# Decode block with gradients on one core: block-diagonal products on VectorE or GpSimd, two rows kept on chip, and a new order of the work

## The chip, the cores and the metric

The kernel runs on one core of a Trainium2 chip. The core has five engines that run beside each other: PE (TensorE, matrix products into PSUM), DVE (VectorE), ACT (ScalarE), POOL (GpSimd) and SP (SyncE, which here only issues transfers), and 16 DMA engines that move data between the chip's memory (HBM) and SBUF. PE has a granted clock that the profile reports. The metric is the device time of one execution in microseconds; less is better. A time of the kernel before is a median of 7 runs.

## The reference

The reference is a decode step of a transformer block and its gradient. With `xn = layernorm(x)` (x has 2 rows of 576):

```
q      = xn @ wq                                # 32 heads of 128, one query for each of 2 batches
p      = softmax(q . k_cache / sqrt(128))       # 16 key/value heads of 4096 positions, 2 queries each
out    = x + (p . v_cache) @ wo + ((xn @ w_gate) * (xn @ w_up)) @ w_down
```

It returns `out` (out_0) and, for a given `grad_out`, the gradients to x (out_1), k_cache and v_cache (out_2, out_3), wq, wo (out_4, out_5), w_gate, w_up and w_down (out_6 to out_8). The caches are 2 x 16 x 4096 x 128 in bf16, 33.6 MB each, the five weights some 25 MB together. Each is read once, and a gradient of the same size is written: 92.5 MB in and 92.5 MB out. Every one of these large gradients is an outer product of small vectors: that of a value cache is `p` times the gradient of the head's output `dO`, that of a key cache is `dscore` times `q`, and so on.

## The kernel before

**Steps.** The work on the caches goes in 16 steps: a step is a pair of key/value heads (index g, 8 pairs) for one of the 2 batches. A step s loads four tiles of 1 MB (keys and values of two heads, [128, 4096] in bf16). DVE transposes each in two halves into an X tile (`t32`, L411); PE multiplies the transposed tile with the queries (`score`, L1094) for the scores, and the transposed values with dO for the gradient of p; ACT and DVE make softmax out of it (`softmax`, `dscore`), and PE spreads the results so that DVE can transpose them into `pp` (probabilities) and `dd` (gradients of the scores). PE then contracts `pp` with the values and `dd` with the keys (`contract`, L1270), which gives the head's output and the gradient of q.

**Outer products.** The gradient of a cache tile comes from `head_outer` (L1116): the probabilities (or `dd`) of 32 rows at a time against a block-diagonal tile `BD` of [128, 16 x 128], eight units of two matmuls for the tiles of one kind in a step, four for a tile of 1 MB. Each unit fills a PSUM bank pair `o` (three of these), and ACT or DVE evicts it (L415 on ACT, L417 on DVE: 128x1024) into a store tile `st`; after four units the tile is full and goes out as one store. The BD tile is made by `build_BD` (L1082): a vector of 128 columns, repeated 16 times, times a mask. Of BD there are three buffers, and 32 are made, two a step. In the kernel before all run on POOL.

**Weights.** For each pair of heads, `group_front` makes q and dO from wq and wo, and `group_back` makes the gradients of wq and wo and adds to the sums `acc` (for out_0) and `accx` (for out_1) once both steps of the pair are done. The MLP goes in nine blocks of 512 columns (`mlp`), with w_gate and w_up in one buffer `gu`. The products with transposed weights for the gradient of x are `dxn` (L619, L624). At the end `final_out` and `final_dx` put the two small rows out_0 and out_1 together: small matmuls into PSUM, a copy by ACT and DVE, a store by SP. Both load x or grad_out once more for this (`rows_in`, L1315), into a slot of the cache tiles, after the last step is done.

**The order.** The program is written in one fixed order, and each engine runs its instructions in that order. The order comes from a planner in the file (`Order`), which runs while the program is built: every part of the work is a generator that yields requests (an instruction on an engine with its cost, a slot of a ring, an event, a transfer), and at each point the planner takes the request that can start first, or, within `SLACK` of it on that engine, the one with the lowest priority number. `pr(name, s)` gives the priorities from the tables `PR`, `HEAD` and `TAIL`. An `EV` request may go to ACT or to DVE, whichever the planner has free first, with `BIAS` against DVE. Slots of the 16 large tiles (`big`) are shared by cache loads (`kv`), transposed tiles (`X`) and store tiles (`st`), with at most `CAP` of each. `MLP0`, `MLPD`, `WQ0` and `WO0` are gates: how many cache loads must have been issued before a weight load may be. A release (`REL`) tells the planner that a slot is free; the waits of the instructions themselves come from the data that they read and write and don't depend on it.

**Queues.** SP issues the cache loads, the 1 MB stores of out_2 and out_3, and the loads of w_down. POOL issues the other weight loads and the stores of the weight gradients, between its own products and copies. Both queues run in program order, so an entry that waits holds those behind it.

Of the kernel before, what the change touches and what calls it, by code (L numbers as in the profile page):

```python
# [9 lines left out]
ALU = mybir.AluOpType  # L10
# [3 lines left out]
P = 128  # L14
# [244 lines left out]
def REL(tag, i):  # L259
    return ("rel", tag, i)  # L260
# [6 lines left out]
def SET(event):  # L267
    return ("set", event)
# [10 lines left out]
def DMA(engine, cost, nbytes, row=8192):  # L279
# [6 lines left out]
CAP = {"kv": 10, "X": 4, "st": 13}  # L286
MLP0, MLPD = 2, 6.27
KVSTORE = "SP"
WQ0, WO0 = -5, -1
LATENCY, DRY = {"SP": 0.5, "ACT": 0.5, "POOL": 0.57}, 0.4  # L290
CLK = 2.0
BIAS = 0.75
SLACK = {"PE": 7.32, "ACT": 0.55, "DVE": 0.31, "POOL": 15.19, "SP": 3.02}
STEP = 28.0
HEAD = {"turn0": 17.8, "turn1": 0.2, "att": -28.9, "dsc": -22.6, "con": 54.2, "conv": 27.6, "out1": 765.1, "out0": -38.2, "back": 3.6, "W0": 24.5, "W1": 17.4, "BD1": -60.5, "BD0": -0.4, "load": 44.6}
TAIL = {"turn0": 16.5, "att": -37.0, "dsc": 7.4, "con": 10.1, "conv": 23.3, "front": -7.7, "back": -49.2, "W0": -13.1, "BD1": 46.3, "BD0": 16.2, "load": 10.1}
PR = {"turn0": 251.3, "turn1": -133.7, "att": -710.4, "dsc": -747.2, "conv": 239.7, "con": 610.6, "out1": 325.7, "out0": 528.9,
      "front": 180.3, "back": 121.7, "W0": 240.0, "W1": 442.5, "BD1": 461.1, "BD0": -51.3, "mlp": -407.4, "wout": -21.9,
      "store": -410.4, "load": 1664.4, "wload": -328.4, "fin": -68.4, "const": -85.8, "mload": -265.1}
# [8 lines left out]
def kernel(  # L308
# [206 lines left out]

    def front():
        xb, yb = st_t[0][0:2, 0:D], st_t[0][0:2, D:2 * D]
# [83 lines left out]
        yield REL("st", 0)  # L601
# [229 lines left out]
    steps = [dict(done=[Event(), Event()], outs=[Event(), Event()], sm=Event(), spread=Event()) for _ in range(NS)]  # L831
# [62 lines left out]
    def group_back(g):  # L894
# [60 lines left out]
        yield SET(left[1].pop())  # L955
        yield REL("qd", st["qs"])
# [107 lines left out]
    def build_BD():  # L1064
        for s in range(NS):
            g, b = divmod(s, Bq)
            for t in (1, 0):
# [13 lines left out]
                yield POOL(3.6)  # L1081
                nc.gpsimd.tensor_tensor(BD_t[i][:], view(vr_t[v][:], 0, P, 0, [[0, 16], [1, Dh]]),  # L1082
                                        view(mask16[:], 0, P, 0, [[1, 16], [0, Dh]]), ALU.mult)
# [47 lines left out]
    def outer(s, t, tag, slot, pr2):  # L1131
# [4 lines left out]
        yield WAIT(*done)  # L1136
# [66 lines left out]
    def dscore(s):  # L1203
# [24 lines left out]
        yield REL("m", k)  # L1228
        S["dd"] = yield ACQ("dd")
# [23 lines left out]
    def contract(s, t):  # L1253
# [11 lines left out]
        for part in range(2):  # L1265
            yield PE(0.427, 0.112, kind="c")
            for k in range(8 * part, 8 * part + 8, 2):
                for j in range(4):
# [3 lines left out]
                                     start=(k == 0), stop=(k == NCH // 2 - 2))  # L1272
        yield SPAWN(free_kv(s, t), pr("con", s))
# [19 lines left out]
    od.used["st"] = 4  # L1293
    for j in range(4):
        od.slots["big"][j] = None
# [145 lines left out]
```

## Time and profile before

| | |
|---|---|
| time, median of 7 runs | 481.8 us (480.3 to 484.5) |
| the profiled execution's own time | 482.92 us |
| its span, first to last instruction | 481.2 us |
| mean granted clock of PE | 0.66 |
| moved by DMA | 185.98 MB, mean 387 GB/s |
| block-diagonal products on POOL (L1082) | 32 of 3600 ns |
| evictions of 128x1024 | ACT 266 of 1033 ns, DVE 42 of 1212 ns |
| half-tile transposes on DVE | 128 of 1222 ns |

In lines of the profile a line number is that of kernel.py as before; `big` are the 16 large tiles, `ps_o` and `ps_m` the PSUM banks for units and for small results. "DMA share" is the mean busy share of the 16 DMA engines in a stretch. A time in brackets behind an instruction is the idle time of its engine just before, and what ended it. SPq is SP's queue of transfers.

### The profile page before, as it was taken

Reading aid. Unit: us, or ns where it says so; the run is one execution under the profiler, and the core shown is the slowest. Engines: PE = TensorE matmul, PEld = TensorE weight load, DVE = VectorE, ACT = ScalarE, POOL = GpSimd, SP = SyncE. Lnnn points to the kernel's source line nnn. Section 1 sums busy time; section 2 is a strip of 40 time slices with the busy share of each in tenths; the row PEclk is TensorE's granted clock in tenths of the full one; section 3 lists DMA queues with packets and bytes.
Section 4 is the critical chain, followed back from the end, with each engine's and each line's share of the span. In section 5 each row is a group of like instructions: output and inputs, shape, how many; then the busy total and the mean of one; then the engine's idle time right before and its main releaser. Section 6 shows DMA issues by size and latency. Waiting matters only on the chain.

```text
span 481.2 us, 15470 instructions
## 1 busy us (share of the span) xinstructions
PE 380.9 (79%) x6570; PEld 233.9 (49%) x6570; DVE 340.8 (71%) x650; ACT 348.4 (72%) x535; POOL 244.6 (51%) x348
## 2 busy tenths in 40 slices
PE   0578679789779958898969889758868698877896
PEld 0445455466446534555545555435544355544634
DVE  5787676666768846788577865758877558786762
ACT  6058658759666749797978789747768589786892
POOL 6464577148642708854673445385492333473411
PEclk9997675657655667657855676656676657566655
DMA  7999999999999999999999999999999999999675
GB/s 273 382 385 406 383 392 397 388 422 404 379 411 347 311 414 422 392 369 422 420 397 407 418 421 419 412 414 414 424 417 400 414 417 422 406 395 400 238 302 207
DMA packets 33455, 185.98 MB, mean 387 GB/s; under 512 B 5038, under 2 KB 5178, under 8 KB 17002
## 3 DMA queue, kind: packets, MB, share of 16 engines
q1 hardware_dynamic: 19874, 139.61, 71.4%
q0 software_dynamic: 13504, 45.38, 25.2%
q8 instruction: 51, 0.84, 0.7%
q14 instruction: 18, 0.15, 0.1%
q10 hardware_dynamic: 8, 0.00, 0.0%
HBM read 92.48 MB, written 92.48 MB: 384 GB/s over the span
## 4 chain that ended last, share of the span: by engine, by line
DMA 40%; PE 27%; DVE 13%; ACT 9%; issue 7%; POOL 3%; SPq 0%; POOLq 0%; DVEq 0%; ACTq 0%
DMA out_dram<-big 19%; DMA gu<-in_B_w_up_dram 12%; DVE big L411 8%; ACT big L415 8%; PE ps_o L1116 5%; PE ps_m L1094 5%; PE ps_m L1270 5%; DMA big<-in_A_v_cache_dram 4%; DMA ww<-in_A_wq_dram 3%; PE ps_m L755 3%; DMA big<-in_A_k_cache_dram 2%; PE ps_o L661 1%; POOL out_dram L641 1%; PE ps_m L619 1%; PE ps_m L796 1%
## 5 line engine op out<-in xcount | busy, mean ns | idle before, releaser
L415 ACT CAST big<-ps_o 128x1024 bf16<-128x1024 f32 (+1 forms) x330 | 292.8, 960 | 39.3 <-PE ps_o L1116 27.1
L411 DVE STREAM_TRANSPOSE big<-big 128x1024 f32<-128x1024 f32 x128 | 154.2, 1222 | 19.3 <-DMA out_dram<-big 10.3
L1082 POOL TENSOR_TENSOR BD<-vr,mask 128x2048 bf16<-128x2048 bf16 x32 | 115.2, 3600 | 81.6 <-ACT vr L415 39.6
L1094 PE MATMUL ps_m<-big,W 128*32 128x128 bf16 x2048 | 58.5, 298 | 6.1 <-POOL W L1059 2.4
L417 DVE CAST big<-ps_o 128x1024 bf16<-128x1024 f32 (+1 forms) x46 | 53.9, 1172 | 10.0 <-PE ps_o L1116 8.6
L1116 PE MATMUL ps_o<-BD,dd 32*128 32x512 bf16 x256 | 52.4, 541 | 9.3 <-ACT big L415 6.2
L1094 PEld LDWEIGHTS <-W 128*32 128x32 bf16 x2048 | 51.2, 135 | 15.4 <-issue 11.5
L1116 PE MATMUL ps_o<-BD,pp 32*128 32x512 bf16 x256 | 51.9, 543 | 7.9 <-POOL BD L1082 3.9
L641 POOL DMA_DIRECT2D out_dram<-big x43 | 33.3, 775 | 38.8 <-ACT big L415 25.1
L1059 POOL COPY W<-rep 32x16 bf16<-32x16 bf16 x128 | 24.6, 192 | 31.3 <-DVE rep L862 25.8
L411 DVE STREAM_TRANSPOSE big<-ww 128x1152 f32<-128x1152 f32 x25 | 34.0, 1360 | 8.9 <-DMA out_dram<-big 5.0
L1270 PE MATMUL ps_m<-big,pp 128*32 128x256 bf16 x512 | 28.8, 381 | 5.4 <-DVE pp L411 3.3
L1270 PE MATMUL ps_m<-big,dd 128*32 128x256 bf16 x512 | 28.0, 360 | 1.6 <-DVE rep L862 0.7
L411 DVE STREAM_TRANSPOSE big<-gu 128x1024 f32<-128x1024 f32 x18 | 21.6, 1226 | 7.8 <-DMA out_dram<-big 3.6
L641 POOL DMA_DIRECT2D out_dram<-tl x26 | 14.7, 568 | 21.4 <-ACT tl L415 13.5
L612 POOL COPY wt<-wm 64x128 bf16<-64x128 bf16 (+1 forms) x34 | 8.9, 262 | 30.7 <-DVE wm L606 29.6
L1270 PEld LDWEIGHTS <-pp 128*32 128x32 bf16 x512 | 15.7, 127 | 13.8 <-DVE pp L411 5.4
L1116 PEld LDWEIGHTS <-dd 32*128 32x128 bf16 x256 | 11.7, 100 | 20.9 <-issue 17.7
L661 PEld LDWEIGHTS <-xnr 32*128 32x128 bf16 x416 | 16.7, 118 | 9.8 <-issue 8.8
L415 ACT CAST sp<-ps_m 128x256 bf16<-128x256 f32 x29 | 11.1, 381 | 14.1 <-PE ps_m L1102 13.9
L1116 PEld LDWEIGHTS <-pp 32*128 32x128 bf16 x256 | 10.8, 99 | 20.6 <-issue 16.8
L661 PE MATMUL ps_o<-hb,xnr 32*128 32x128 bf16 x288 | 17.4, 280 | 2.9 <-ACT big L415 2.1
(207 smaller groups left out, 559.2 us busy)
## 6 DMA issues: line engine op xcount, KB each, us to landing
out_dram<-big SPq DMA_DIRECT2D x64, 1024.0 KB, 16.1
big<-in_A_k_cache_dram SPq DMA_DIRECT2D x32, 1024.0 KB, 10.9
big<-in_A_v_cache_dram SPq DMA_DIRECT2D x32, 1024.0 KB, 17.1
out_dram<-big POOLq DMA_DIRECT2D x26, 512.0 KB, 12.2
out_dram<-big POOLq DMA_DIRECT2D x17, 576.0 KB, 9.8
ww<-in_B_w_down_dram SPq DMA_DIRECT2D x9, 576.0 KB, 7.5
ww<-in_A_wo_dram POOLq DMA_DIRECT2D x8, 576.0 KB, 17.1
gu<-in_B_w_gate_dram POOLq DMA_DIRECT2D x9, 512.0 KB, 14.9
```

The costliest lines, as they stand in the source:

```text
L411: nc.vector.transpose(out, in_)
L415: nc.scalar.copy(out, in_)
L417: nc.vector.tensor_copy(out=out, in_=in_)
L612: nc.gpsimd.tensor_copy(view(Wt[:], 64 * h, 64, 0, [[dims[-1][1], n], [1, dims[-1][1]]]), view(Wm[:], 64 * h, 64, off, dims))
L641: (nc.gpsimd if engine == "POOL" else nc.sync).dma_start(dst, src)
L661: nc.tensor.matmul(o[:, aa, dc * P:(dc + 1) * P], lhsT=xnr[32 * a:32 * a + 32, dc * P:(dc + 1) * P], rhs=rhs(a), start=True, stop=True)
L755: nc.tensor.matmul(dh, lhsT=Wdy[:, e, 2 * k:2 * k + P], rhs=view(X[:], 0, P, 64 * k + e, [[D, FC], [2, 32]]), start=(k == 0 and e == 0), s ...
L1059: nc.gpsimd.tensor_copy(view(W_t[t][w][:], 32 * a, 32, 6 + 8 * a, [[G * WW, 4], [WW, G], [1, 2]]), view(rep_t[grp[g]["qs"]][:], 32 * a, 32 ...
L1082: nc.gpsimd.tensor_tensor(BD_t[i][:], view(vr_t[v][:], 0, P, 0, [[0, 16], [1, Dh]]), view(mask16[:], 0, P, 0, [[1, 16], [0, Dh]]), ALU.mult)
L1094: nc.tensor.matmul(sc[32 * cq:32 * cq + 32, :], lhsT=view(W[:], 0, P, (be * G + l) * WW + 6 - 4 * c2 - 2 * l, [[1, 32]]), rhs=view(X[:], 0 ...
L1116: nc.tensor.matmul(o[:, k, :], lhsT=pr2[32 * c4:32 * c4 + 32, :], rhs=BD[32 * c4:32 * c4 + 32, 8 * l + 4 * h2:8 * l + 4 * h2 + 4, :], star ...
L1270: nc.tensor.matmul(ct[32 * j:32 * j + 32, 0:2 * P], lhsT=view(rT, 0, P, 4 * c + 2 * l, [[1, 32]]), rhs=kv_t[kvS[s][t][l]][:, Dh * c:Dh * ( ...
```

## The change

- `build_BD`: the product may go to POOL (cost 3.6 in the planner's table) or to DVE (2.25, with a bias of 1.5 x `BIAS`), whichever is done first by the planner's times. In the order that results, 21 of the 32 are on POOL and 11 on DVE.
- x and grad_out are read once at the start into a tile of their own, `xy`, which stays; the final rows use it and write their results into it. The second loads are gone, the final parts no longer wait for the last step but for the sums, and the store slot 0 is free from the start.
- Releases in the planner stand behind all readers: the slots of `pp`, `dd` and `BD` are released after the contraction too (`ct`), that of `qd` after the block-diagonal tiles, and the second spread waits for the first one's.
- The tables are other ones: caps, gates, bias, slack and all priorities. So the whole order is another one; 21 POOL products, 221 instead of 214 evictions of 128x2x512 on ACT and 35 instead of 42 on DVE are in it. The arithmetic of every part is the same.

```diff
--- before.py
+++ after.py
@@ -283,20 +283,20 @@
 
 
 NBIG, NGU, NWW, NBD = 16, 1, 5, 3
-CAP = {"kv": 10, "X": 4, "st": 13}
-MLP0, MLPD = 2, 6.27
+CAP = {"kv": 8, "X": 7, "st": 11}
+MLP0, MLPD = 5, 7.05
 KVSTORE = "SP"
-WQ0, WO0 = -5, -1
+WQ0, WO0 = -2, 3
 LATENCY, DRY = {"SP": 0.5, "ACT": 0.5, "POOL": 0.57}, 0.4
 CLK = 2.0
-BIAS = 0.75
-SLACK = {"PE": 7.32, "ACT": 0.55, "DVE": 0.31, "POOL": 15.19, "SP": 3.02}
+BIAS = 0.68
+SLACK = {"PE": 0.09, "ACT": 0.54, "DVE": 0.79, "POOL": 28.11, "SP": 7.69}
 STEP = 28.0
...
 
 
 def pr(name, s):
@@ -513,8 +513,10 @@
     def carve(t, n):
         return pairs(t[:])[0:2, D * n:D * (n + 1)]
 
+    xy = const.tile([2, 2 * D], BF16, name="xy")
+
     def front():
-        xb, yb = st_t[0][0:2, 0:D], st_t[0][0:2, D:2 * D]
+        xb, yb = xy[:, 0:D], xy[:, D:2 * D]
         for t, src in ((xb, A_x), (yb, grad_out)):
             yield DMA("ACT", 0.45, 2304, 1152)
             nc.scalar.dma_start(t, src.rearrange("b s d -> (b s) d"))
@@ -598,7 +600,6 @@
             nc.vector.tensor_tensor(xnT[:], xnT[:], view(nrT[:], 0, P, k, [[0, 6], [1, 2]]), op)
         nc.vector.memset(gg[:, 0], 0.0)
         yield REL("m", i)
-        yield REL("st", 0)
         yield SET(Eprep)
 
     def stationaries(i, rep, npos, half):
@@ -828,7 +829,7 @@
 
 
     grp = [dict(Lm=Event(), Eq=Event(), Ed=Event(), Lq=Event(), Lo=Event(), EoT=Event()) for _ in range(NG)]
-    steps = [dict(done=[Event(), Event()], outs=[Event(), Event()], sm=Event(), spread=Event()) for _ in range(NS)]
+    steps = [dict(done=[Event(), Event()], outs=[Event(), Event()], ct=[Event(), Event()], sm=Event(), spread=Event()) for _ in range(NS)]
 
     def group_front(g):
         st = grp[g]
@@ -953,6 +954,7 @@
         nc.vector.tensor_add(accx[:], accx[:], m_t[m][:, 0:160])
         yield REL("m", m)
         yield SET(left[1].pop())
+        yield WAIT(*bE[2 * g], *bE[2 * g + 1])
         yield REL("qd", st["qs"])
         yield WAIT(*E)
         yield REL("R", r)
@@ -1078,9 +1080,10 @@
                 cp(e, vr_t[v][:], m_t[m][:, 0:P])
                 yield REL("m", m)
                 i = yield ACQ("BD")
-                yield POOL(3.6)
-                nc.gpsimd.tensor_tensor(BD_t[i][:], view(vr_t[v][:], 0, P, 0, [[0, 16], [1, Dh]]),
-                                        view(mask16[:], 0, P, 0, [[1, 16], [0, Dh]]), ALU.mult)
+                e = yield ("any", [("POOL", 3.6, 0.0), ("DVE", 2.25, 1.5 * BIAS)])
+                (nc.gpsimd if e == "POOL" else nc.vector).tensor_tensor(
+                    BD_t[i][:], view(vr_t[v][:], 0, P, 0, [[0, 16], [1, Dh]]),
+                    view(mask16[:], 0, P, 0, [[1, 16], [0, Dh]]), ALU.mult)
                 yield REL("vr", v)
                 bS[s][t] = i
                 yield SET(bE[s][t])
@@ -1133,7 +1136,7 @@
         done = [Event() for _ in range(4 * G)]
         for l in range(G):
             yield SPAWN(head_outer(s, t, l, pr2, done[4 * l:4 * l + 4]), pr(f"out{t}", s))
-        yield WAIT(*done)
+        yield WAIT(*done, steps[s]["ct"][t])
         yield REL("BD", bS[s][t])
         yield REL(tag, slot)
         yield SET(steps[s]["outs"][t])
@@ -1226,6 +1229,7 @@
         nc.vector.scalar_tensor_tensor(out=c["ds"][:], in0=dp, scalar=c["cr"][:], in1=c["pr"][:],
                                        op0=ALU.subtract, op1=ALU.mult)
         yield REL("m", k)
+        yield WAIT(S["spread"])
         S["dd"] = yield ACQ("dd")
         m = yield ACQ("m")
         yield PE(0.107, 0.052)
@@ -1270,6 +1274,7 @@
                     nc.tensor.matmul(ct[32 * j:32 * j + 32, 0:2 * P], lhsT=view(rT, 0, P, 4 * c + 2 * l, [[1, 32]]),
                                      rhs=kv_t[kvS[s][t][l]][:, Dh * c:Dh * (c + 2)],
                                      start=(k == 0), stop=(k == NCH // 2 - 2))
+        yield SET(S["ct"][t])
         yield SPAWN(free_kv(s, t), pr("con", s))
         ob, cs = osb_t[i][:].rearrange("p w n -> p (w n)"), ct[:, 0:2 * P]
         e = yield EV(256)
@@ -1290,8 +1295,8 @@
         yield REL("m", m)
         yield SET(S["done"][t])
 
-    od.used["st"] = 4
-    for j in range(4):
+    od.used["st"] = 3
+    for j in range(1, 4):
         od.slots["big"][j] = None
 
     for g in range(NG):
@@ -1308,34 +1313,23 @@
             yield PRIO(pr("front", 2 * g))
             yield from group_front(g)
 
-    def rows_in(src):
-        i = yield ACQ("kv")
-        t = kv_t[i]
-        yield DMA("SP", 0.36, 2304, 1152)
-        nc.sync.dma_start(t[0:2, 0:D], src.rearrange("b s d -> (b s) d"))
-        e = Event()
-        yield ("lset", e)
-        return t, e
-
-    def rows_put(o, t, out):
-        nc.scalar.copy(view(t[:], 0, 2, D, [[P, 5], [1, 64]]), o[0:2, 0, 0:320].rearrange("p (k n) -> p k n", k=5))
-        nc.vector.tensor_copy(view(t[:], 0, 2, D + 64, [[P, 4], [1, 64]]), o[0:2, 1, 0:256].rearrange("p (k n) -> p k n", k=4))
-        nc.sync.dma_start(out.rearrange("b s d -> (b s) d"), t[0:2, D:2 * D])
-
-    def rows_add(o, t):
+    def rows_put(o, n, out):
+        nc.scalar.copy(view(xy[:], 0, 2, n * D, [[P, 5], [1, 64]]), o[0:2, 0, 0:320].rearrange("p (k n) -> p k n", k=5))
+        nc.vector.tensor_copy(view(xy[:], 0, 2, n * D + 64, [[P, 4], [1, 64]]), o[0:2, 1, 0:256].rearrange("p (k n) -> p k n", k=4))
+        nc.sync.dma_start(out.rearrange("b s d -> (b s) d"), xy[:, n * D:(n + 1) * D])
+
+    def rows_add(o, n):
         for k in range(2):
             nc.tensor.matmul(o[0:2, k, 0:320 - 64 * k], lhsT=ident[0:2, 0:2],
-                             rhs=view(t[:], 0, 2, 64 * k, [[P, 5 - k], [1, 64]]), start=True, stop=False)
+                             rhs=view(xy[:], 0, 2, n * D + 64 * k, [[P, 5 - k], [1, 64]]), start=True, stop=False)
 
     def final_out():
         yield PRIO(PR["fin"])
-        yield WAIT(*steps[NS - 1]["done"])
-        t, e = yield from rows_in(A_x)
-        yield WAIT(e, *acc_E)
+        yield WAIT(Eprep, *acc_E)
         i = yield ACQ("o")
         o = o_t[i]
-        yield PE(0.5, 0.5)
-        rows_add(o, t)
+        yield PE(1.1, 0.5)
+        rows_add(o, 0)
         for dc in range(5):
             r = slice(0, P) if dc < 4 else slice(64, P)
             for k in range(2):
@@ -1348,14 +1342,12 @@
         yield ACT(0.4)
         yield DVE(0.4)
         yield DMA("SP", 0.3, 2304, 1152)
-        rows_put(o, t, out_0)
+        rows_put(o, 0, out_0)
         yield REL("o", i)
 
     def final_dx():
         yield PRIO(PR["fin"])
-        yield WAIT(*steps[NS - 1]["done"])
-        t, e = yield from rows_in(grad_out)
-        yield WAIT(e, Eprep, *accx_E)
+        yield WAIT(Eprep, *accx_E)
         i = yield ACQ("o")
         o = o_t[i]
         m = yield ACQ("m")
@@ -1366,7 +1358,7 @@
         for k in range(2):
             nc.tensor.matmul(mt[0:32, 8:12], lhsT=accx[:, P:160], rhs=F8[:, 4 * k:4 * k + 4],
                              start=(k == 0), stop=(k == 1))
-        rows_add(o, t)
+        rows_add(o, 1)
         yield DVE(0.5)
         nc.vector.tensor_copy(g[:, 0:8], mt[:, 0:8])
         nc.vector.tensor_copy(g[0:32, 8:12], mt[0:32, 8:12])
@@ -1391,7 +1383,7 @@
         yield ACT(0.4)
         yield DVE(0.4)
         yield DMA("SP", 0.3, 2304, 1152)
-        rows_put(o, t, out_1)
+        rows_put(o, 1, out_1)
         yield REL("o", i)
 
     od.spawn(front(), -1000.0)
```

## The prediction

> **What bounds the kernel now.** I read the page first, then the busy time by stretches, then the waits of SP's queue, then the timeline of the last 40 us. The page (engines; DMA in 40 slices; queues):
>
> ```profile
> span 481.2 us, 15470 instructions
> ...
> PE 380.9 (79%) x6570; PEld 233.9 (49%) x6570; DVE 340.8 (71%) x650; ACT 348.4 (72%) x535; POOL 244.6 (51%) x348
> ...
> DMA  7999999999999999999999999999999999999675
> ...
> q1 hardware_dynamic: 19874, 139.61, 71.4%
> q0 software_dynamic: 13504, 45.38, 25.2%
> ```
>
> No engine is above 79%, but the DMA engines are full in all slices except the first and the last three, and their two large queues fill 96.6% of the span. So the bytes (186 MB) bound the middle, and time can only go where the DMA engines pause or run at a lower rate. Stretches of 3 us over the whole span give these pauses (share below 1, times 3 us): 3.1 us at the start, 0.6 us at 57, 2.0 us in 153 to 165, 0.15 us at 210, and 12.1 us from 444 to 480. The columns are busy time by engine, granted clock, DMA share, GB/s:
>
> ```profile
> 57.00:60.00 3.00, 1.12 (x9) 0.23 (x5) 3.00 (x6) 3.00 (x4) 1.13 (x2) 0.50 0.81 278
> 153.00:156.00 3.00, 2.46 (x37) 1.59 (x40) 3.00 (x6) 2.41 (x8) 0.59 (x2) 0.50 0.76 257
> 156.00:159.00 3.00, 3.00 (x70) 2.37 (x62) 2.47 (x6) 2.59 (x4) 1.67 (x3) 0.50 0.70 265
> ```
> ```profile
> 445.00:450.00 5.00, 3.54 (x35) 2.46 (x33) 3.78 (x7) 4.31 (x6) 3.27 (x1) 0.76 0.33 138
> 455.00:460.00 5.00, 5.00 (x92) 2.82 (x85) 3.07 (x7) 4.33 (x6) 1.88 (x4) 0.50 0.65 225
> 465.00:470.00 5.00, 4.61 (x78) 2.86 (x76) 3.43 (x6) 5.00 (x8) 1.25 (x3) 0.50 0.96 394
> ```
>
> In the pauses PE, ACT and DVE are busy: DMA waits there for evictions. Every 1 MB store of the two cache gradients, and every cache load, goes through SP's one queue in program order, so a store that isn't ready holds all that stands behind it. SP's waits:
>
> ```profile
> SPq L641 <- ACT big L415: 126.6, 40, 9.9
> SPq L641 <- DVE big L417: 91.7, 22, 14.0
> SPq L984 <- DMA out_dram<-big: 62.3, 17, 10.4
> ```
>
> The 14.0 us is the store at 158.8: behind it stood two loads, and that is the pause at 153. The third line is loads that wait until an earlier store has emptied their slot. Last, the end:
>
> ```profile
> 442.11 1.90 PE L1270 MATMUL ps_m<-big,pp 128*32 128x256 bf16 x31 [1.92 <-DMA big<-in_A_v_cache_dram]
> 462.70 1.06 SPq L1315 DMA_DIRECT2D big<-in_A_x_dram  x1
> 470.71 0.63 PE L1327 MATMUL ps_o<-big,ident 2*2 2x320 bf16 x2
> 471.27 1.87 PE L1343 MATMUL ps_o<-identf,acc 128*2 128x64 f32 x16
> 473.37 0.50 PEld L1365 LDWEIGHTS ps_m<-F,accx 128*128 128x128 f32 x2 [0.21 <-issue]
> 475.35 4.01 SPq L1323 DMA_DIRECT2D out_dram<-big  x2
> ```
>
> The last value tiles are there at 442.1. The 39.1 us after that are a stage of their own: nine 1 MB stores and the last weight gradients still have to be evicted (ACT busy 22.6 of the 25 us from 445 to 470), and then the two small rows come out one behind the other.
>
> **The change part by part.** The sum goes against the profiled execution: 482.9 us, its span of 481.2 and 1.7 around it; it lies 1.1 us above the median of 481.8.
>
> *The final rows.* The last add into accx ends at 470.18. PE then does the out_0 row (470.71 to 473.44), and only then (473.37) starts the grad row, whose chain of small matmuls and vector steps runs to 479.07 and lands by 481.2. In the changed order the out_0 matmuls stand ahead of the last dxn product, where PE waits for ACT's evictions anyway; two outer-product units (0.61 us each, as at 470.04) stand in their place. The gap of 3.2 us falls to some 1.5: gain 1.7. Bounds: 0, if these units wait for their PSUM banks, and 2.7, all of the out_0 work. The last large store empties the DMA engines at about 477, 4 us before the end, so it does not take over.
>
> *x and grad_out kept.* Two 2.2 KB loads go, with 2.1 us of SP's queue (462.70 to 464.84). The store behind them (464.94) had its last eviction at 464.38, so 0.5 us at most; DMA at 465 to 470 is 0.96 full. I take 0. At the start the same rows are read into another tile: nothing moves.
>
> *The evictions of the end.* I counted what stands in each engine's order behind the product of the last value tiles (L1270 before, L1274 after). ACT before: 20 evictions of 128x1024 and 8 of 128x576; after: 18 and 6. With 1.033 and 0.657 us each (the group rows by shape) ACT has 3.4 us less. DVE goes from 4 large ones to 6 and one of 576 (1.212 and 0.745 us): 3.2 us more, on an engine that is 70% busy there. Stores behind that point on SP: nine in both. Gain between 0 and 3.4; I take 2, since ACT is the fuller engine.
>
> *Block-diagonal products.* In the changed order 11 of 32 leave POOL for DVE. POOL loses 11 x 3.6 = 39.6 us that cost little (PE's outer products wait 3.9 us for them in the group row of pp; POOL itself idles 81.6 us ahead of them). On DVE the trace has no such product. Two-input rows of 128, 160 and 256 columns (280, 310, 415 ns) give about 1.05 ns per column and 0.145 fixed: 2.3 us for 2048 columns, 25 us in all, which takes DVE from 71% to 76%. From below, the rate of the transpose (1222 ns for 1024 f32, the same bytes) gives 1.2 us each and 13 us; from above, POOL's own 3.6 and 40 us. I take 2.3, the nearest operation. Covers: DVE's 140 idle us and the full DMA queues; cost 0. If the cover is gone, a product holds the transposes, evictions and softmax steps behind it on DVE: 2.3 us each time, 25 in all at worst. The one for the last step stands right ahead of that step's softmax maximum, and 6.6 MB of stores, weights and values lie on SP between the landing of its keys and of its values, some 17 us at 400 GB/s: covered.
>
> Here a rule speaks against the change. The trace: all 32 products on POOL take 3600 ns, and transposes (one input from SBUF) keep their 1222 beside them; nothing with two long SBUF inputs on DVE is in it. The Trainium skill (SBUF — State Buffer, "SBUF: two separate sides") says that a VectorE operation with two SBUF inputs and a GpSimd operation that reads SBUF exclude each other for the whole instruction. By that, each of the 11 could wait for a POOL product, 11 x 3.6 = 40 us more on DVE at worst as an estimate, of which its idle time would hide about half, so that the sum would end near 498 instead of 478; no run shows it yet. The sum goes without it.
>
> *Slots released behind all readers.* These are releases in the planner's book-keeping; no instruction carries them. They only change the order chosen. Waits of DVE for a reader on PE of a slot it rewrites are small now (4.4 us for L1270 in all): 0.
>
> *The order.* On SP, 13 cache transfers before reuse a slot whose previous store stands at most 5 MB ahead in the same queue, one directly ahead (the slot behind the pause at 57); after it is 8, none nearer than 2 MB. That is for the third wait line, 62.3 us, of which little pauses DMA. Against it: SP has 10 cache loads and one weight load ahead of its first store instead of 12 and one, POOL 2.8 instead of 3.4 MB; at 390 GB/s this lasts to about 40 us instead of 47. The first store went out at 35.2 and should again, but soon a load waits for that store's slot. I take +1 there and -0.5 for the pauses of the middle (bounds -2.7, all of them, and +17, below).
>
> Sum: -1.7 - 2 + 1 - 0.5 = -3.2: span 478.0, profiled time 479.7; 1.1 lower as the median: 478.6. The predicted time is **478.5 us**, 0.7% less.
>
> **The rivals.**
> 1. *Fuller DMA, 465 to 474.* From 12 to 132 us the engines are full but move 394 GB/s (mean of ten stretches), later (252 to 433) 413. Weight loads in short pieces come early now; in the changed order the MLP blocks begin later and reach further. If the first 120 us ran at the later rate, 120 x (1 - 394/413) = 5.5 us go, and 2.7 of pauses: 478.6 - 8 = 470. Against it: the bytes and pieces are the same in sum.
> 2. *Nothing to tell, 479.4 to 484.2.* The shorter end is given back by one pause like that at 153 (2 us) or a head that runs dry for 3.
> 3. *Slower, 485 to 498: store runs on SP.* The changed SP queue has a run of five stores and one of six with no load between; before, four is the longest. A store needs four evictions, 4.1 us of ACT at 1.033, while DMA moves it in 2.6; where its tile isn't filled in advance, each loses 1.5, eleven of them 17 us. The pool lets stores hold 11 slots instead of 13 and loads 8 instead of 10, so less stands ready. It decides from about five unready stores on (7.5 us, more than the 3.2 gained and the 2.4 that can't be told). The store that held SP for 14.0 us speaks for it; that the lead of loads over stores stays between 7 and 16 tiles in both orders (14 at most before) against.
>
> That the change does not do what it says is out: the order shows the 11 products on DVE and no late loads.
>
> **How the numbers follow.** A measurement of this kernel can tell about 0.5% (2.4 us) from no change. Forecast, the end shorter and the middle as before (474 to 479.4): 0.35. Fuller DMA: 0.18. Nothing to tell: 0.18. Store runs or another held queue: 0.29. Faster 0.53, same 0.18, slower 0.29. The range 467 to 492 leaves out the lowest of rival 1 (0.04) and the top of rival 3 (0.1); the forecast's own is 474 to 480.5.
>
> **What would show it.** Right: the out_0 matmuls ahead of the last dxn, under 2 us from the last accx add to the first grad matmul, some 35 us from the last value tiles to the end, DVE products near 2.3 us, DMA pauses of the middle no longer than 3 us. Wrong: slices in the middle under 9 tenths of DMA with SP waiting for evictions (rival 3); a first slice past 40 us that runs dry; products of 3 us and more on DVE, or POOL products above 3.6 (the lock); the last values landing later than 443.

## The result, and the profile after

The changed kernel takes 488.5 us (median of 12 runs, 486.35 to 492.0), the kernel before 482.5 us beside it (31 runs, 479.85 to 485.19). The ratio is 1.013, 95% interval 1.011 to 1.016: slower by 1.3%, where 0.7% faster was predicted. The profiled execution took 486.9 us with a span of 485.1, 3.9 more than that of before, so the trace holds 3.9 of the 6.0 us between the medians.

The page after (engines; DMA and GB/s in 40 slices; the two large queues):

```profile
span 485.1 us, 15445 instructions
...
PE 378.1 (78%) x6570; PEld 231.6 (48%) x6570; DVE 364.4 (75%) x660; ACT 349.6 (72%) x536; POOL 208.6 (43%) x337
...
DMA  7999999999999999999999999999999999999775
GB/s 270 380 378 422 407 351 386 418 391 352 381 407 419 401 404 402 416 383 390 410 409 381 374 417 419 378 415 372 419 410 391 414 422 422 341 388 414 280 309 191
...
q1 hardware_dynamic: 19866, 139.61, 72.2%
q0 software_dynamic: 13504, 45.38, 24.7%
```

The work moved as announced: DVE up by 23.6 us, POOL down by 36. The DMA row is as full as before. But q1 needs 72.2% of 485.1, that is 350.2 us of 16 engines, for the same 139.61 MB that took 71.4% of 481.2, or 343.6; q0 went from 121.3 to 119.8. Together the transfers kept the engines some 5 us longer. Most of the time is lost with the engines full, and the share of DMA can't show that: only its rate can.

The trace has every packet. An 8 KB packet of q1 takes 309 ns at the median in both kernels, but 320 on average before and 327 after; 16384 of them on 16 engines make 6.8 us. With all packets at their medians (309, 178 and 159 ns for 8, 4.5 and 4 KB) the traffic would take 446.4 us in every kernel here. The span is that floor, plus what packets take beyond it, plus the rest (engines without work, less the overlap of two queues): before 446.3 + 22.3 + 12.6, after 446.4 + 27.1 + 11.7.

In bytes, counted from the packets: until 108 us the two kernels move the same. The changed one loses 1.0 MB by 120, is ahead by 1.1 MB at 216 (the pause of the kernel before at 153 is gone), and loses 0.85 at 261 to 279, 1.0 at 306 to 342 and 0.8 at 405 to 441. At 441 it is 2.2 MB behind, 5.7 us at its mean rate of 383 GB/s, and the end then takes some 1.8 us less. The places of the loss, by stretches, after (busy time by engine, clock, DMA share, GB/s):

```profile
108.00:111.00 3.00, 2.90 (x99) 2.10 (x97) 2.27 (x7) 2.75 (x4) 1.14 (x6) 0.96 0.80 317
114.00:117.00 3.00, 2.22 (x74) 1.59 (x75) 3.00 (x5) 0.95 (x3) 3.00 (x2) 1.00 0.98 281
156.00:159.00 3.00, 3.00 (x37) 1.27 (x39) 2.62 (x3) 2.18 (x3) 2.92 (x4) 0.50 1.02 417
261.00:264.00 3.00, 3.00 (x92) 2.28 (x90) 2.49 (x7) 2.88 (x4) 3.00 (x3) 0.50 0.94 321
339.00:342.00 3.00, 3.00 (x44) 1.42 (x36) 2.02 (x6) 1.87 (x2) 0.00 (x0) 0.50 0.94 365
420.00:423.00 3.00, 3.00 (x82) 2.24 (x80) 2.40 (x4) 2.95 (x6) 1.87 (x3) 0.50 0.98 291
```

And three of the same stretches before:

```profile
114.00:117.00 3.00, 2.25 (x48) 1.56 (x48) 2.37 (x3) 3.00 (x4) 1.89 (x5) 0.50 1.01 409
339.00:342.00 3.00, 3.00 (x46) 2.32 (x46) 2.02 (x5) 1.83 (x3) 1.53 (x8) 0.58 1.01 426
420.00:423.00 3.00, 1.09 (x35) 0.69 (x33) 3.00 (x4) 2.45 (x4) 2.46 (x8) 0.99 1.06 381
```

The last two columns are the reading: shares of 0.94 and 0.98 with 281 to 365 GB/s after, 1.01 and 1.06 with 381 to 426 before. Only the row at 108 is a pause (0.80), and the row at 156 shows that the old one at 153 is gone. The 8 KB packets are long just there:

| stretch, us | mean 8 KB packet before, ns | after, ns |
|---|---|---|
| 112 to 120 | 313 | 364 |
| 259 to 273 | 322 | 360 |
| 308 to 318 | 318 | 357 |
| 336 to 342 | 310 | 363 |
| 420 to 426 | 340 | 389 |

What stands ahead of such a stretch is in SP's timeline after (start, length, line, transfer, count):

```profile
108.78 3.61 SPq L642 DMA_DIRECT2D out_dram<-big  x2
112.50 1.33 SPq L986 DMA_DIRECT2D big<-in_A_k_cache_dram  x2
113.94 1.67 SPq L986 DMA_DIRECT2D big<-in_A_v_cache_dram  x2
```

SP stood before a store until 112.06 while its queue ran out; then five transfers of 1 MB went out within 3.6 us, and the packets of the next microseconds are the long ones. How far SP is ahead can be counted: the bytes it has issued that have not yet moved. Between 10 and 440 us these are 3.39 MB on average before and 2.89 after. Less than 2.1 MB, two tiles, lie ahead for 101 us before and 126 after. Nearly nothing (under 0.1 MB) for 15.2 us before and 5.5 after: the changed queue runs dry less often, but is short more often. Counted by what lay ahead when a packet's transfer was issued, 8 KB packets of the changed kernel took 353 ns on average behind less than 1.05 MB (1875 packets) and 323 behind more; before it was 335 (1520 packets) and 318. By what lies ahead at the moment there is no such order: in the stretch at 336 to 342 it is 4.6 MB on average.

SP's waits after:

```profile
SPq L642 <- ACT big L415: 159.0, 42, 14.6
SPq L642 <- DVE big L417: 59.7, 22, 7.0
SPq L986 <- DMA out_dram<-big: 53.0, 14, 10.3
SPq L986 <- PE ps_m L1274: 20.4, 4, 7.4
SPq L986 <- PE ps_m L1097: 16.8, 8, 8.2
```

Over all rows the waits of stores stay the same (262 us before, 256 after). Cache loads wait 141 us instead of 111, and what grew is loads that wait for PE to have read their slot (28 us before, 71 after), with 8 slots for loads instead of 10. The loads of w_down in the same queue wait 9 us instead of 37, so SP waits 406 us in all where it waited 410: not more, but at other places.

### The profile page after: what moved, and what is told of

Its sections match the earlier page's. It is cut to its first block, busy times and chain, and to the rows that moved or that the text cites. A ratio compares the mean times of both kernels' runs of the same rounds, so it can differ in the third digit from the quotient of the medians.

```text
span 485.1 us, 15445 instructions
## 1 busy us (share of the span) xinstructions
PE 378.1 (78%) x6570; PEld 231.6 (48%) x6570; DVE 364.4 (75%) x660; ACT 349.6 (72%) x536; POOL 208.6 (43%) x337
## 3 DMA queue, kind: packets, MB, share of 16 engines
q1 hardware_dynamic: 19866, 139.61, 72.2%
## 4 chain that ended last, share of the span: by engine, by line
DMA 38%; PE 29%; ACT 13%; DVE 13%; issue 5%; POOL 2%; SPq 0%; DVEq 0%; ACTq 0%; POOLq 0%
DMA out_dram<-big 24%; ACT big L415 11%; DVE big L411 8%; PE ps_o L1119 6%; DMA ww<-in_A_wq_dram 5%; PE ps_m L1097 5%; PE ps_m L1274 4%; DMA big<-in_A_k_cache_dram 4%; DMA ww<-in_B_w_down_dram 4%; PE ps_m L879 2%; PE ps_m L756 2%; DVE big L417 1%; PE ps_m L620 1%; PE ps_o L676 1%; PE ps_o L662 1%
## 5 line engine op out<-in xcount | busy, mean ns | idle before, releaser
L415 ACT CAST big<-ps_o 128x1024 bf16<-128x1024 f32 (+1 forms) x335 | 296.4, 957 | 50.6 <-PE ps_o L1119 31.8
L1084 POOL TENSOR_TENSOR BD<-vr,mask 128x2048 bf16<-128x2048 bf16 x21 | 75.6, 3599 | 46.5 <-ACT vr L415 34.4
L1119 PE MATMUL ps_o<-BD,dd 32*128 32x512 bf16 x256 | 54.6, 523 | 13.8 <-ACT big L415 10.6
L1097 PE MATMUL ps_m<-big,W 128*32 128x128 bf16 x2048 | 61.2, 286 | 5.0 <-issue 1.1
L1097 PEld LDWEIGHTS <-W 128*32 128x32 bf16 x2048 | 48.2, 127 | 18.8 <-issue 16.5
L1119 PE MATMUL ps_o<-BD,pp 32*128 32x512 bf16 x256 | 49.7, 546 | 6.8 <-ACT big L415 5.0
L417 DVE CAST big<-ps_o 128x1024 bf16<-128x1024 f32 (+1 forms) x41 | 48.6, 1189 | 8.4 <-PE ps_o L1119 4.1
L642 POOL DMA_DIRECT2D out_dram<-big x43 | 33.3, 774 | 46.9 <-ACT big L415 23.8
L613 POOL COPY wt<-wm 64x128 bf16<-64x128 bf16 (+1 forms) x34 | 10.9, 320 | 71.7 <-DVE wm L607 68.8
L1084 DVE TENSOR_TENSOR BD<-vr,mask 128x2048 bf16<-128x2048 bf16 x11 | 25.2, 2286 | 1.2 <-PE ps_o L662 0.7
L756 PE MATMUL ps_m<-big,Wdy 128*128 128x128 bf16 x162 | 16.0, 275 | 5.9 <-DVE big L411 3.7
```

The costliest lines, as they stand in the source:

```text
L415: nc.scalar.copy(out, in_)
L417: nc.vector.tensor_copy(out=out, in_=in_)
L613: nc.gpsimd.tensor_copy(view(Wt[:], 64 * h, 64, 0, [[dims[-1][1], n], [1, dims[-1][1]]]), view(Wm[:], 64 * h, 64, off, dims))
L642: (nc.gpsimd if engine == "POOL" else nc.sync).dma_start(dst, src)
L756: nc.tensor.matmul(dh, lhsT=Wdy[:, e, 2 * k:2 * k + P], rhs=view(X[:], 0, P, 64 * k + e, [[D, FC], [2, 32]]), start=(k == 0 and e == 0), s ...
L1084: (nc.gpsimd if e == "POOL" else nc.vector).tensor_tensor(BD_t[i][:], view(vr_t[v][:], 0, P, 0, [[0, 16], [1, Dh]]), view(mask16[:], 0, P, ...
```

## The experiments

Three theories. A: something systematic in the changed rules and constants costs the 1.3% (the smaller cap for loads, or the runs of stores of rival 3). B: the products on VectorE cost it, by their time or by excluding GpSimd. C: the planner's order jumps with any of its inputs; both kernels hold orders that happen to be short, and the changed one's is a little longer.

### Products back on GpSimd, order kept

```diff
-                (nc.gpsimd if e == "POOL" else nc.vector).tensor_tensor(
+                nc.gpsimd.tensor_tensor(
```

> The changed kernel with its order kept instruction for instruction, but the 11 block-diagonal products that it runs on VectorE (11 x 2.29 us) run on GpSimd (11 x 3.6 us) at the same places. Theory A (the re-made order holds the SP queue; the products cost nothing): 1.010 to 1.017 times the kernel before, at most 1.5 us better than the changed kernel. Theory B (the 25 us of products on VectorE, or an exclusion between VectorE and GpSimd, are the loss): 0.993 to 1.004. Theory C (the planner's tables and the planner's rules form one draw; any other pairing scatters): as A for this run.

Measured: 488.4 us, ratio 1.012 (1.007 to 1.017), the same as the changed kernel. Its row:

```profile
L1084 POOL TENSOR_TENSOR BD<-vr,mask 128x2048 bf16<-128x2048 bf16 x32 | 115.2, 3601 | 44.6 <-DVE vr L417 18.5 <-ACT vr L415 17.1 <-DMA out_dram<-big 5.9
```

and in the changed kernel:

```profile
L1084 POOL TENSOR_TENSOR BD<-vr,mask 128x2048 bf16<-128x2048 bf16 x21 | 75.6, 3599 | 46.5 <-ACT vr L415 34.4
L1084 DVE TENSOR_TENSOR BD<-vr,mask 128x2048 bf16<-128x2048 bf16 x11 | 25.2, 2286 | 1.2 <-PE ps_o L662 0.7
```

The 25.2 us on DVE, and 39.6 us taken from POOL, are worth nothing in either direction. B falls.

### Code and constants crossed

The planner's constants (from the caps to the priorities) of one kernel in the code of the other; the edit is the first block of the change, alone or left out.

> The kernel before (all products on GpSimd, x and grad_out loaded again, old release rules) planned with the constants of the changed kernel (caps kv 8, X 7, st 11, MLP blocks from load 5 on, its priorities). Theory A, in the form that the constants carry the loss: 1.010 to 1.025. Theory B: 0.995 to 1.004, since no product runs on VectorE. Theory C: any pairing that the constants were not fitted to is worse than either kernel: 1.015 to 1.04.

> The changed code (products on either engine, x and grad_out kept on chip, new release rules, out_0 before the last dxn) planned with the constants of the kernel before (caps kv 10, X 4, st 13, its priorities). Theory A: 0.990 to 1.000, the shorter end without the loss of the middle. Theory B: 1.008 to 1.018, since products still go to VectorE. Theory C: 1.01 to 1.04, the constants being fitted to the other code.

Measured: old code with new constants 501.4 us, 1.040 (1.036 to 1.043); new code with old constants 516.2 us, 1.068 (1.063 to 1.072). In the first the old release rules let part of out_2 be made from tiles that are written again too early; the number and size of the instructions is the same. Both are slower than either kernel: against A in both forms, and as C expects, though the second lies above C's range as well (1.04).

### Stores from ScalarE's queue

```diff
-                (nc.gpsimd if engine == "POOL" else nc.sync).dma_start(dst, src)
+                (nc.gpsimd if engine == "POOL" else nc.scalar).dma_start(dst, src)
```

> The changed kernel with its order kept, but the 64 large stores of out_2 and out_3 are issued from ScalarE's queue at their places in the order instead of SyncE's, so that a store that waits for its evictions holds no load behind it (it holds ScalarE instead, when VectorE's eviction is the late one). Theory A with stores as the holders of SP (rival 3 of the prediction; waits of 59.0 + 31.5 us at the store line): 0.985 to 1.003. Theory A with loads held by slots in use (cap kv 8): 1.008 to 1.015. Theory B: 1.010 to 1.020.

Measured: 507.8 us, 1.052 (1.048 to 1.056), outside of all three. SP has no stores to stand before, and its loads now wait 140.8 us for stores to empty their slots (53.0 in the changed kernel) and 79.6 us for DVE's transposes (2.4). On ACT's queue the stores themselves wait little, 9.9 us in all and 1.4 at most, and their 64 issues take 21.8 us of its sequencer. How the time is lost in this run stays open.

### The old caps

```diff
-CAP = {"kv": 8, "X": 7, "st": 11}
+CAP = {"kv": 10, "X": 4, "st": 13}
```

> The changed kernel planned with the slot caps of the kernel before (kv 10, X 4, st 13 instead of 8, 7, 11), all other constants as changed. Reading so far: time goes with how long the SP queue has less than one cache tile (1.05 MB) issued and not yet moved: between 10 and 440 us 35 us in the kernel before, 43 in the changed one, 85 and 88 in the two crossed kernels. Theory A (fewer slots for loads are what leaves the queue short): 0.990 to 1.004, and the short time back to 35 us or less. Theory C (each plan is a draw of its own, and one constant out of its set gives a worse one): 1.015 to 1.07, short time 55 to 90 us.

The short times named there came from a count in which some issues stood twice. Counted once, less than 1.05 MB lie ahead for 46.6 us before, 39.9 after, 67.5 and 85.1 in the crossed kernels: this tells the slow kernels from the others, but not these two from each other. Under 2.1 MB does (101 and 126; 138 and 184).

Measured: 521.2 us, 1.079 (1.076 to 1.081), 107.5 us under one tile. With the old caps the order comes out 6.5% longer than the changed kernel's, and above C's range (1.07) as well. It is another order throughout, so this run doesn't tell what the cap alone is worth; the orders planned anew below, with the caps as they are, scatter as widely.

### Stores behind the next load

On SP alone: the large store is held back while the program is written, and issued behind the next cache load or ahead of the first that takes its slot.

```diff
+                if engine == "SP" and row == 8192 and len(issued_n) < 4 * NS:
+                    od.late.append((slot, dst, src))
...
                     nc.sync.dma_start(kv_t[i][:], views[t][b, G * g + l])
+                    issued_n.append(n)
+                    late()
```

> The changed kernel with the order of PE, ACT, DVE and POOL untouched; on SP alone each large store is moved behind the next cache load, unless that load takes the store's own slot. Theory A with stores as the holders (rival 3 of the prediction): the loads no longer stand behind unready stores, short time under 35 us, 0.990 to 1.005. Theory A with slots as the holders: the slots are freed one load later, the loads wait longer, 1.015 to 1.04.

Measured: 526.9 us, 1.089 (1.084 to 1.093). The loads' wait for stores (L1001 is the load here):

```profile
SPq L1001 <- DMA out_dram<-big: 171.9, 19, 25.0
```

One place later for each store, with four engines untouched, costs 7.4% against the changed kernel. The slots are what runs short: a store that comes late gives its slot late, and a load then holds SP for longer than the store would have.

### The two long runs of stores split

The run of five stores becomes three, two loads, two; the run of six becomes four, two loads, two; on SP alone. The two that are held back join the stores that follow, so that the longest run ahead of the end is four, as in the kernel before.

> The changed kernel with PE, ACT, DVE and POOL untouched; on SP alone the run of five stores becomes three, two cache loads, two, and the run of six becomes four, two loads, two. Rival 3 of the prediction (runs of stores hold the loads; the changed kernel loses 0.8 MB, 2 us, against the one before at 261 to 279, right behind the run of six): 1.003 to 1.010. If the loads need slots that the stores free: 1.015 to 1.03.

Measured: 494.9 us, 1.026 (1.022 to 1.031), 1.3% above the changed kernel. So rival 3's store runs are not the loss. They are issued at 144 to 165 and at 179 to 196 us, within or next to the stretch from 153 to 216 in which the changed kernel gains 1.8 MB on the one before; the stretch at 261 isn't right behind them, as the expectation has it. That the loads behind them need the slots fits the range named for it, but is not shown: the loads' wait for stores is 45.9 us here, 53.0 in the changed kernel.

### Planned anew

The smallest changes of a planner's input that give another order, first for the changed kernel, then for the one before:

```diff
-CLK = 2.0
+CLK = 2.01
```

> The changed kernel with the planner's cost of all PE work raised by half a per cent (2.0 to 2.01 us per us at full clock): no rule, cap or priority differs, only the order that comes out. Theory A (something systematic in the changed rules and constants costs the 1.3%): 1.009 to 1.018. Theory C (the order is a draw): outside of this, anywhere from 1.00 to 1.06, with the short time to match.

> The changed kernel with the planner's cost of PE work lowered by half a per cent (2.0 to 1.99). Theory A (systematic): 1.009 to 1.018. Theory C (each order a draw, and the two kernels hold orders that were kept because they are short): 1.02 to 1.06.

> The changed kernel with the handicap at 0.69 instead of 0.68. If the changed rules and constants cost 1.3% as such: 1.009 to 1.018. If its order is a kept draw as well: 1.02 to 1.06, like its neighbours (1.024 and 1.051).

> The kernel before with the planner's cost of all PE work raised by half a per cent. Theory A: 0.997 to 1.004. Theory C: 1.01 to 1.06, since the order of the kernel before would be a draw that was kept because it is short.

> The kernel before with the planner's cost of PE work at 1.99 instead of 2.0. If the old rules and constants give short orders in general: 0.997 to 1.010. If its order is a kept draw: 1.02 to 1.06, like its neighbour at 2.01 (1.046).

> The kernel before with the planner's handicap of VectorE for evictions at 0.74 instead of 0.75 (the order differs from PE's 1427th of 12910 rows on). General: 0.997 to 1.010. Draw: 1.02 to 1.06.

> The kernel before with that handicap at 0.78 (the order is the same up to PE's row 5784 of 12910, and differs behind it). General: 0.997 to 1.010. Draw, over the second half alone: 1.005 to 1.04.

In the last three the old release rules again let tiles be written ahead of a reader, so that parts of out_2 and out_4 (twice) and of out_3 and out_5 hold other values, with the same instructions. The account of the result's section for these runs and those above (not for the stores from ScalarE's queue, which use another DMA queue):

| order | ratio to before | span | packets beyond 446.4 | rest | under 2.1 MB ahead, us |
|---|---|---|---|---|---|
| before | 1 | 481.2 | 22.3 | 12.6 | 101 |
| changed | 1.013 | 485.1 | 27.1 | 11.7 | 126 |
| old order, new end | 1.002 | 479.3 | 21.1 | 12.0 | 97 |
| changed, products on GpSimd | 1.012 | 489.0 | 25.8 | 16.8 | 112 |
| changed, two runs split | 1.026 | 493.8 | 29.2 | 18.1 | 123 |
| changed, PE cost 2.01 | 1.024 | 494.0 | 25.2 | 22.5 | 113 |
| changed, PE cost 1.99 | 1.051 | 506.8 | 30.6 | 29.8 | 175 |
| changed, handicap 0.69 | 1.073 | 515.3 | 31.2 | 37.8 | 214 |
| before, PE cost 2.01 | 1.046 | 503.4 | 27.9 | 29.2 | 156 |
| before, PE cost 1.99 | 1.033 | 497.4 | 28.8 | 22.2 | 170 |
| before, handicap 0.74 | 1.079 | 520.8 | 25.3 | 49.0 | 135 |
| before, handicap 0.78 | 1.026 | 495.9 | 25.4 | 24.1 | 125 |
| old code, new constants | 1.040 | 498.2 | 27.5 | 24.1 | 138 |
| new code, old constants | 1.068 | 514.0 | 31.5 | 36.2 | 184 |
| changed, old caps | 1.079 | 519.4 | 36.1 | 36.8 | 179 |
| changed, stores one load later | 1.089 | 524.5 | 42.6 | 35.3 | 188 |

The neighbours of the changed order lie at 1.049 on average, those of the old at 1.046: two families that can't be told apart, each 1 to 8% above its own kernel. So nothing here shows a rule or a constant that costs 1.3% by itself, as A has it, though seven draws that spread over 5% can't exclude one. C fits: each kernel holds an order shorter than all its neighbours, and the two differ by less than the neighbours do among each other. Four runs lie above the ranges that C was given (1.068, 1.073 and twice 1.079). How these two orders were found no run here shows.

The table also says where an order loses. The neighbours lose most in the rest (22 to 49 us, 12 in the two kernels), that is in engines without work; the changed kernel loses against the one before in the packets. A single profile moves by some us in this account: the run with the products on GpSimd takes the time of the changed kernel (488.4 and 488.5 us), but its profiled execution was a long one (490.7), with a rest of 16.8 instead of 11.7.

### The old order with the new end

The last lines of the changed code in the kernel before (x and grad_out kept, no late loads, out_0 ahead of the last dxn). PE's order is the old one up to row 12794 of 12910.

```diff
-        yield WAIT(*steps[NS - 1]["done"])
-        t, e = yield from rows_in(A_x)
-        yield WAIT(e, *acc_E)
+        yield WAIT(Eprep, *acc_E)
```

> The kernel before with its order kept up to PE's last hundred instructions; only the end is the changed one: x and grad_out are kept on chip and written over in place, the two late loads are gone, and the out_0 row stands ahead of the last dxn product. The prediction's first terms, by themselves: 1.7 us (0 to 2.7) for the final rows and 0 to 0.5 for the late loads, so 0.994 to 1.000 of the kernel before, most likely 0.996. If the end is set by something else: 0.999 to 1.003.

Measured: 483.5 us, 1.002 (0.9995 to 1.004): no gain, where 0.996 was most likely. PE at the end of this kernel, and SP:

```profile
458.92 1.05 PE L1272 MATMUL ps_m<-big,dd 128*32 128x256 bf16 x16
465.62 1.87 PE L1334 MATMUL ps_o<-identf,acc 128*2 128x64 f32 x16
468.30 0.62 PE L621 MATMUL ps_m<-big,wm 128*32 128x128 bf16 x16
470.48 0.59 PE L1354 MATMUL ps_m<-F,accx 128*128 128x8 f32 x2
472.64 0.61 PE L1118 MATMUL ps_o<-BD,dd 32*128 32x512 bf16 x2
```
```profile
474.33 0.35 SPq L643 DMA_DIRECT2D out_dram<-big  x1
476.22 0.26 SPq L1316 DMA_DIRECT2D out_dram<-xy  x1
```

From the end of the last contraction (459.97 here, 461.81 before) the grad row starts after 10.5 us instead of 11.6, 1.1 sooner; the dxn itself starts 1.0 later (8.3 instead of 7.3), since the out_0 matmuls now stand ahead of it. But the span ends after 19.3 us as before (19.4). The out_0 row also stands ahead of the last outer product (472.64), whose tile then goes out at 474.33, and its last packet is at 477.86, behind the grad row's (477.8). The row's store stands behind it in the same queue: the last large store has taken over the end.

This run and that with the products on GpSimd leave the order as the cause of the 1.3%: with the changed order kept, the products are worth nothing (1.012 and 1.013), and with the old order kept, the rows on chip and the new end are worth nothing either (1.002); the releases are no instructions.

### Copies alone

The traffic of the caches without computation, with a fixed number of transfers ahead (the edit is a kernel of its own; per stage a loop like this):

```python
def pairs_ahead(k, n):
    q = [load() for _ in range(k)]
    for i in range(n):
        store(q.pop(0))
        if i + k < n:
            q.append(load())
```

> No computation: the cache tiles are only copied to out_2 and out_3 through SBUF on SyncE's queue, in four stages by how much is issued ahead when a store waits for its tile: nothing, one ready store of 1 MB, two transfers, four transfers; then the same four stages with weights copied on GpSimd's queue beside them. In the traces so far packets of 8 KB take 309 ns at the median, but 370 to 430 in the stretches where the changed kernel loses, with the engines shown as full. Theory P (a queue refilled just in time is what makes the packets long): in the first half 340 ns and more with nothing or one transfer ahead, 309 to 318 with two and four. Theory Q (the packets of the other queue make them long): 309 to 318 in all four stages of the first half, 325 and more in all of the second. In the stage with nothing ahead both expect idle engines between the transfers.

Measured, in the first half: with nothing ahead 367 ns for an 8 KB packet, with one ready store 370, with two transfers 333, with four 316. DMA by windows, at 6 to 48, 58 to 92, 104 to 130 and 142 to 168 us: the four stages in this order (packets; queue: packets, MB, share):

```profile
DMA packets 1670, 12.24 MB, mean 291 GB/s; under 512 B 176, under 2 KB 176, under 8 KB 176
q1 hardware_dynamic: 1670, 12.24, 81.9%
...
DMA packets 1653, 12.10 MB, mean 356 GB/s; under 512 B 176, under 2 KB 176, under 8 KB 176
q1 hardware_dynamic: 1653, 12.10, 100.7%
...
DMA packets 1413, 10.32 MB, mean 397 GB/s; under 512 B 153, under 2 KB 153, under 8 KB 153
q1 hardware_dynamic: 1413, 10.32, 101.2%
...
DMA packets 1477, 10.79 MB, mean 415 GB/s; under 512 B 160, under 2 KB 160, under 8 KB 160
q1 hardware_dynamic: 1477, 10.79, 100.4%
```

Stages two to four all show full engines, at 356, 397 and 415 GB/s. With two or four ahead nine packets in ten take 309 to 314 ns; with none or one, every tenth takes 606 or more. The 333 of the third stage mixes two things. Its long packets all start before 111 us, right behind four transfers that went out within 3 us (103.2 to 106.4) when the queue had run down to 0.4 MB. From 111 to 130, with 1.3 MB or more ahead of every issue, each 8 KB packet takes 309 ns (the same view):

```profile
DMA packets 1114, 8.13 MB, mean 428 GB/s; under 512 B 122, under 2 KB 122, under 8 KB 122
q1 hardware_dynamic: 1114, 8.13, 101.2%
```

So P holds, with two transfers ahead enough once they are kept there. Q fails: with GpSimd's queue full beside them (185 to 255 us) the packets took 320 ns even with nothing ahead, so another queue hides the effect; that queue was done at 313, ahead of the last two stages. This fits the stretch at 112 to 120 of the changed kernel, where 368 of 369 packets are SP's and five transfers went out behind an empty queue. In the other four GpSimd's queue is at work too, but by single microseconds the long packets of three of them lie where it moves 0.05 MB or less per us (312 to 314, 337 to 339, 420 to 422), and so do those at 261 to 264. At 268 to 272 it moved 0.44 MB and the packets took some 400 ns all the same. That it is the same effect in these stretches is likely, not shown.

## Why the prediction was wrong, point by point

- **The order (+1 - 0.5).** This step failed, and decided the sign. It looked for time in pauses, stretches with a DMA share below 1, and priced the order by them at 0.5 us in sum; by bytes the changed kernel is 5.7 us behind at 441. The pauses are nearly even: the one at 153 is gone (417 GB/s there now), those at 66, 108 to 114 and 411 to 417 are new, and in stretches of 3 us they make 3.7 us up to 441 where there were 3.1. (The rest of the account fell from 12.6 to 11.7 at the end alone.) What the step put at nothing is the length of a packet: the changed order loses 4.8 us there, mostly at a share of 0.92 and more, and more of its transfers are issued with little ahead. The step's bound of +17 held that; its value did not. The signs named as right came about (0.1 us from the last accx add to the grad matmul, 33 us for the end, products of 2.29 us, no pause of 3 us); none of them looks at the rate. More basic: every neighbour of either order, planned with one constant moved by 0.5 to 4%, lies 1 to 8% above its kernel. That an order made anew costs about nothing has no ground in a trace of the old one.
- **Rival 3 (slower, store runs on SP).** It had the right sign, the right queue, and the smaller cap for loads; its mechanism was wrong. The store waits did not grow (262 and 256 us); the cache loads' did (111 to 141), for slots, while those of w_down fell by about as much; the runs stand where the changed kernel gains, and splitting them costs 1.3% more. Its sign, "middle slices under 9 tenths", does not appear at all.
- **Final rows (-1.7).** The grad row starts 1.1 us sooner in the old order and 1.8 in the changed one (9.7 us from the last contraction, 11.6 before), near the estimate. "It does not take over", said of the last store, was wrong where the step stands alone: worth 0.8 us more (0.2 less to 1.9 more) there. The changed kernel's end, after:

```profile
472.88 0.64 PE L1323 MATMUL ps_o<-xy,ident 2*2 2x320 bf16 x2
473.44 1.87 PE L1337 MATMUL ps_o<-identf,acc 128*2 128x64 f32 x16
475.54 0.62 PE L620 MATMUL ps_m<-big,wm 128*32 128x128 bf16 x16
476.69 0.46 PE L1357 MATMUL ps_m<-F,accx 128*128 128x8 f32 x2
```

From the last contraction (466.97) to the end it takes 18.2 us, 1.2 less than before.

- **The end's evictions (-2).** Together with the rows, the end won some 1.8 us by bytes against 3.7 predicted. From the first contraction of the last values it is 33.3 us (35 predicted, 39.1 before), but this contraction comes at 451.86 instead of 442.11 and waits for the softmax, no longer for the values:

```profile
451.86 1.05 PE L1274 MATMUL ps_m<-big,pp 128*32 128x256 bf16 x16 [1.12 <-DVE pp L411]
```

- **Products on VectorE (0, at 2.3 us each).** Right in size (2286 ns) and in cost. The lock that the Trainium skill states (SBUF — State Buffer, "SBUF: two separate sides") is there: a short copy of GpSimd that starts while such a product runs ends just behind it, whatever its own length; no product of the changed kernel is longer for it (2293 ns at most). After, POOL and then DVE:

```profile
409.28 2.62 POOL L613 COPY wt<-wm 64x128 bf16<-64x128 bf16 x2 [11.35 <-DVE wm L607]
```
```profile
409.13 2.27 DVE L1084 TENSOR_TENSOR BD<-vr,mask 128x2048 bf16<-128x2048 bf16 x1
```

The first of the two copies took 2.27 us instead of 0.29 and ended at 411.55, 0.15 after the product. This met two copies in the whole run, 4.0 us more on POOL, and no product of POOL; what the prediction worked out from the rule, 498 us, needed each of the 11 to meet one. Other orders show the lock between products, and that it is the later one that waits: in the changed kernel planned with the PE cost of 1.99 a product of VectorE that started while one of GpSimd ran took 2599 ns, and in the new code with old constants one of GpSimd behind one of VectorE took 4842 instead of 3600.
- **x and grad_out kept (0), releases (0).** Within what can be told here: the old order with the new end holds the first and gains nothing. The releases cost no time either, but they are no formality. By the diff, the old rules release a pp or dd tile behind the outer products alone, though the contraction reads it too, and four of the five other orders planned with them write a tile too early; which tile, no run shows.
- **Rival 1 (fuller DMA).** The early rate did not rise: at 108 us both kernels have moved 41.0 MB.

## What to carry to other kernels

A DMA share of 1 is not a full DMA: read the rate beside it, and the length of a packet of one size. In the copies alone 8 KB packets take 309 ns where two transfers are kept ahead, and 367 to 370 on average with none or one. And where a planner writes the order, plan the old kernel anew with a constant moved by half a per cent before pricing any change: the spread of these times, here 1 to 8%, is the size of what a re-made order can cost, and a saving of 0.7% lies far within it.

## What was not expected of the hardware

With one 1 MB transfer ahead in the only busy queue, every tenth 8 KB packet takes 606 ns or more, twice the 309 of the median, and the engines count as busy all the time; two transfers kept ahead bring 428 GB/s instead of 356. With the same order, 64 stores of 1 MB moved from SP's queue to ACT's cost 3.8%, though they wait there for 9.9 us in all.
